# First-MoE weights: the low word's shift as a scaled copy on ScalarE, the gates' low halves subtracted on VectorE

## Chip, cores and metric

One core of one Trainium2 chip. The metric is the device time of one execution in microseconds (us), the median of several runs; lower is better. Engines are named as the profile names them: PE is the matrix engine (TensorE), DVE is VectorE, ACT is ScalarE, POOL is GpSimd, SP is SyncE, which here only issues DMAs.

## What is computed

An attention over four batches, then two mixtures of experts ("MoE") on its output. Cut to what matters:

```python
# attention: B, H, S, D = 4, 8, 576, 64; every query sees keys closer than 4, and all pooled keys (means of 4)
out = repeat(softmax(q_d @ k_d.T / 8) @ v_d, 4) + softmax(masked(q @ k.T / 8)) @ v
x = out.transpose(0, 2, 1, 3).reshape(2304, 512)
# first MoE: w1, w2, w3 are 512 x 768 (the gates), w_out is 768 x 512
h = np.maximum(np.maximum(x @ w1, x @ w2), x @ w3)
x = h @ w_out
# second MoE: w_in 512 x 2048, w_out 2048 x 512
h = np.maximum(x @ w_in, 0.0)
y = h * h @ w_out
```

The weights of both MoEs arrive as float64; q, k and v as float32.

## The kernel before

**Decoding a weight.** A float64 weight block of 128 x 512 is loaded as raw 64-bit words into a staging tile `raw` (pool `stg`, three buffers, line 93), and read as two 32-bit words, `low` and `high`. Five steps make two float32 tiles of it, `hi` (a value rounded to the matrix engine's format) and `lo` (what the rounding left):

- L98, DVE: `high` times 2^-112 and cut at a top value, which shifts the exponent to float32's.
- L103, DVE: `low` shifted right by 29, which leaves three bits of mantissa.
- L107, DVE: `high` shifted left by 3, or'ed with `low`.
- L111, DVE: the sign bit of `high` or'ed in. `low` is now the float32 weight.
- L122, ACT: `hi`, a copy of `low`; then L123, POOL: `lo`, the difference of `low` and `hi`. When `lo` is done the staging buffer is free, and SP, which waits for that at L94, issues the load of the third next weight. SP works through its loads in order, so the loads of q, k, v behind a waiting one wait too.

The first MoE has 24 such blocks: 18 of the gates (`g<f><g>`, f from 0 to 5, gate g from 0 to 2) and 6 of `w_out` (`o1<f>`). Each product with a weight is three matmuls (`mm3`, lines 128 to 130): hi times hi, hi times lo, lo times hi.

**Order.** The instructions of PE stand in the order of a plan written as tokens (`CFG`). The plan "first" runs the attention of batch 0 with all 18 gate weights decoded in between (`d1`), and puts in the first gate products as soon as a slice of x is there. "second" holds the gates and outputs of batch 0, the attention of batch 1, and the six `w_out` blocks; "mid" (twice) and "last" follow, and then the second MoE in six tiles. On DVE, ACT, POOL and SP a scheduler sets the order from its own estimates until "last"; from there on DVE's order is the written one too. Each engine works through its queue in order.

**Names in the rows.** `s`, `sd` are scores in PSUM, `sm` and `pd` the softmax of the windowed and the pooled part, `mx` and `sms` its maxima and sums, `pt` and `ptd` the transposed softmax, `o` the attention's output in PSUM, `x32` its sum with the pooled part (`up`), `xhi` and `xlo` its two halves. `g` is a gate's product in PSUM, `c` the running maximum over the gates (L380, L382), `hh` and `hl` its halves. Behind a name stand batch, head pair and part (`F` first blocks, `B` the others).

On POOL stand, beside L123: sums for pooling q, k, v (L193 to L195, L203, L204), softmax normalisation (L260, L261) and the low half of h (L388).

Of the kernel before, what the change touches and what calls it, by code (L numbers as in the profile page):

```python
# [8 lines left out]
F32 = mybir.dt.float32  # L9
F32R = mybir.dt.float32r  # L10
U32 = mybir.dt.uint32
U64 = mybir.dt.uint64
AF = mybir.ActivationFunctionType
ALU = mybir.AluOpType
# [4 lines left out]
P = 128  # L19
NEG = -1.0e9  # L20
REBIAS = 2.0**-112
F32_TOP = struct.unpack("f", struct.pack("I", (254 << 20) | 0xFFFFF))[0]

# The order of issue, as plans of tokens. Attention of a batch, per head pair p: l load q and k, m load v
# for pooling, p pool q and k, w pool v; per part F (first blocks) or B (the others): n load the windows of
# v, s scores and softmax, t transposes, v products with v. c loads the constants, d decodes a weight of the
# first MoE, e one of the second, k<kc> adds a slice of the first gate. G<half><f> and Y<half><d> are tiles
# of the gates and of y. In "second" and "mid" the attention is that of the next batch.
# "t0" counts the weights decoded at each step of the first tile of the second MoE; "qpool" gives the engine
# (v or p) that pools q and k of the first batch, "mult", "evac", "xlo" those of (later, first) batches.  # L30
CFG = {
    "qpool": "vvvp",
    "mult": "vp",
# [26 lines left out]
def local_global_attention__then__moe_kernel(  # L60
    ctx: ExitStack, tc: tile.TileContext, qT, kT, vP, cst, wg, wo1, wi2, wo2, out
):
    nc = tc.nc
    B, NP, _, S = qT.shape
# [18 lines left out]
    stg = ctx.enter_context(tc.tile_pool(name="stg", bufs=3))  # L83
# [3 lines left out]
        for b in range(B)  # L87
    ]

    def split_weights(items, late=False):  # L90
        work = []
        for src, name, *_ in items:
            raw = stg.tile([P, 512], U64, tag="raw", name=f"raw_{name}")
            nc.sync.dma_start(out=raw, in_=src)  # L94
            words = raw.bitcast(U32).rearrange("p (n two) -> p n two", two=2)
            work.append((words[:, :, 0], words[:, :, 1]))
        for low, high in work:
            nc.vector.tensor_scalar(  # L98
                out=high.bitcast(F32), in0=high.bitcast(F32), scalar1=REBIAS, scalar2=F32_TOP,
                op0=ALU.mult, op1=ALU.min,  # L100
            )
        for low, high in work:
            nc.vector.tensor_scalar(  # L103
                out=low, in0=low, scalar1=29, scalar2=None, op0=ALU.logical_shift_right
            )
        for low, high in work:
            nc.vector.scalar_tensor_tensor(  # L107
                out=low, in0=high, scalar=3, in1=low, op0=ALU.logical_shift_left, op1=ALU.bitwise_or
            )
        for low, high in work:  # L110
            nc.vector.scalar_tensor_tensor(  # L111
                out=low, in0=high, scalar=0x80000000, in1=low, op0=ALU.bitwise_and, op1=ALU.bitwise_or
            )
        parts = []
        for (src, name, pool, tag, bufs), (low, high) in zip(items, work):
            w = low.bitcast(F32)
            hi = pool.tile([P, 512], F32R, tag=tag, name=f"hi_{name}", bufs=bufs)
            lo = pool.tile([P, 512], F32R, tag=tag, name=f"lo_{name}", bufs=bufs)
            if late:
                nc.vector.tensor_copy(hi, w)  # L120
            else:
                nc.scalar.activation(out=hi, in_=w, func=AF.Copy)  # L122
            nc.gpsimd.tensor_tensor(out=lo, in0=w, in1=hi.bitcast(F32), op=ALU.subtract)  # L123
            parts.append((hi, lo))
        return parts

    def mm3(ps, whi, wlo, xhi, xlo, first, last):
        nc.tensor.matmul(ps, whi, xhi, start=first, stop=False)  # L128
        nc.tensor.matmul(ps, whi, xlo, start=False, stop=False)  # L129
        nc.tensor.matmul(ps, wlo, xhi, start=False, stop=last)  # L130
# [7 lines left out]
    at = ExitStack()  # L138
    ap = at.enter_context(tc.tile_pool(name="ap", bufs=2))
    ps_a = at.enter_context(tc.tile_pool(name="ps_a", bufs=4, space=PSUM))  # L140
    ps_m = p1.enter_context(tc.tile_pool(name="ps_m", bufs=4, space=PSUM, side="right"))

    const = ap.tile([P, NMASK * WIN + P], F32, name="const", bufs=1)
    mask = const[:, 0 : NMASK * WIN]
# [205 lines left out]
    w1_t = {}  # L350
    wo_pool = []
    w1_todo = [("g", f, g) for f in range(NF1) for g in range(NG)] + [("o", f, 0) for f in range(NF1)]

    def load_w1(n=2):
        keys = w1_todo[:n]
        del w1_todo[:n]
        items = [
            (wg[f, g], f"g{f}{g}", wpool, "w", 36) if kind == "g" else (wo1[f], f"o1{f}", wo_pool[0], "wo", 12)
            for kind, f, g in keys
        ]  # L360
        if items:
            w1_t.update(zip(keys, split_weights(items)))

    h_t = {}

    def gate_mm(b, h, f, g, ps, kc, first, last):
# [3 lines left out]
        ks = slice(kc * P, (kc + 1) * P)  # L370
        mm3(ps[:, 0:N], hi[:, ks], lo[:, ks], xhi[:, kc, :], xlo[:, kc, :], first, last)

    def gate_ps(b, h, f, g):
        return ps_m.tile([P, 512], F32, tag="m", name=f"g{b}{h}{f}{g}")

    def gate_max(b, h, f, g, ps, c):
        N = HALF[h][1] * QB
# [14 lines left out]
    def gate_unit(b, h, f):  # L392
        c = None
        for g in range(NG):
            ps = gate_ps(b, h, f, g)
            for kc in range(NP):
                gate_mm(b, h, f, g, ps, kc, kc == 0, kc == NP - 1)
            c = gate_max(b, h, f, g, ps, c)

    def y_unit(b, h, d):  # L400
        N = HALF[h][1] * QB
        ps = ps_m.tile([P, 512], F32, tag="m", name=f"yp{b}{h}{d}")
        for f in range(NF1):
            hi, lo = w1_t["o", f, 0]
            ds = slice(d * P, (d + 1) * P)
            mm3(ps[:, 0:N], hi[:, ds], lo[:, ds], h_t[b, h, f][0], h_t[b, h, f][1], f == 0, f == NF1 - 1)
        ys = tmp.tile([P, 320], F32, tag="c", name=f"ys{b}{h}{d}")[:, 0:N]
        nc.scalar.activation(out=ys, in_=ps[:, 0:N], func=AF.Copy)
        nc.scalar.dma_start(out=yscr[b][h][:, d, :], in_=ys)
# [4 lines left out]
    def act_on(b, token):  # L414
# [4 lines left out]
        elif kind == "c":  # L419
            nc.sync.dma_start(out=const, in_=cst)  # L420
        elif kind == "m":
            att_load_v(b, p)
        elif kind == "n":
            att_load_w(b, p, part)
        elif kind == "p":
            att_pool(b, p)
        elif kind == "w":
            att_pool_v(b, p)
        elif kind == "s":
            att_scores(b, p, part)  # L430
        elif kind == "t":
            att_trans(b, p, part)
        elif kind == "v":
            att_pv(b, p, part)
            vdone.add((b, p, part))
        elif kind == "d":
            load_w1(p)
        elif kind == "G":
            assert all(states[0, i].get("fdone") for i in range(NP))
            assert token[1] == "0" or len(vdone) == 2 * NP  # L440
            gate_unit(0, int(token[1]), int(token[2]))
        elif kind == "k":
            assert states[0, p]["fdone"]
            kc_done.append(p)
            for g in range(NG):
                gate_mm(0, 0, 0, g, g0[g], p, len(kc_done) == 1, len(kc_done) == NP)
                if len(kc_done) == NP:
                    c0[0] = gate_max(0, 0, 0, g, g0[g], c0[0])

    w2_t = {}  # L450
    w2_todo = [(kind, f) for f in range(NF2) for kind in ("i", "o")]

    def load_w2(n=1):
        keys = w2_todo[:n]
        at = 2 * NF2 - len(w2_todo)
        del w2_todo[:n]
        items = []
        for i, (kind, f) in enumerate(keys):
            where = (w2, "w2", 12) if at + i < 6 else (wpool, "w", 36) if at + i < 24 else (gp, "w2", 16)
            items.append(((wi2 if kind == "i" else wo2)[f], f"{kind}2{f}", *where))  # L460
        if items:
            w2_t.update(zip(keys, split_weights(items, True)))

    yt = {}
    NT2 = NT // T2
# [22 lines left out]

    with tc.manual_schedule(engines={ENG.PE}):
        g0 = [gate_ps(0, 0, 0, g) for g in range(NG)]  # L490
        c0 = [None]
        kc_done = []
# [6 lines left out]
        def run(b, plan):  # L499
            for token in plan.split():  # L500
                kind = token[0]
                if kind == "G":
                    gate_unit(b, int(token[1]), int(token[2]))
                elif kind == "Y":
                    y_unit(b, int(token[1]), int(token[2]))
                elif kind == "e":
                    load_w2()
                elif kind == "d":
                    load_w1(1)
                else:  # L510
                    act_on(b + 1, token)
# [119 lines left out]
```

## Time and profile before

| | before |
|---|---|
| median of 3 runs | 888.01 us (887.69 to 888.41) |
| span of the profiled execution | 886.9 us |
| PE busy | 834.2 us, 94% of the span |
| DVE busy | 492.7 us, 56% |
| ACT busy | 265.7 us, 30% |
| POOL busy | 238.8 us, 27% |
| chain that ended last | PE 76%, DVE 18%, issue 3%, the rest 1% or less each |

The profile is of one execution. The shares are means over stages with different limits: PE is all but full after the first sixth of the span, and DVE is full inside it. The chain is followed back from the last instruction, at each step to what released it.

### The profile page before, as it was taken

The numbers are of one execution on the slowest core, as the hardware profiler recorded it, in microseconds if no ns is written. First come the engines' busy times: TensorE is split into PE (matmuls) and PEld (weight loads), VectorE is DVE, ScalarE is ACT, GpSimd is POOL, SyncE is SP. The second block draws the span as 40 slices with busy tenths as digits, with TensorE's granted clock in tenths as the row PEclk, the third lists the DMA queues.
The fourth block names the chain that finished last, engine by engine and source line by source line (L and its number), as shares of the span: only waits on it lengthen the run. The fifth ranks groups of instructions, "written<-read, shape, count | busy, mean of one in ns | idle before, by whom it ended". The sixth has DMA issues, their size and how long they took to land.

```text
span 886.9 us, 15362 instructions
## 1 busy us (share of the span) xinstructions
PE 834.2 (94%) x6160; PEld 770.2 (87%) x6160; DVE 492.7 (56%) x944; ACT 265.7 (30%) x645; POOL 238.8 (27%) x278
## 2 busy tenths in 40 slices
PE   5558987999999999998998999999999999999998
PEld 4447986999999999998998888889989998999896
DVE  7999998633764256668679986223223223222222
ACT  3334333322343123421112434223223223223222
POOL 4877674520433005024124433001001001000000
PEclk9678999999999999999999999999999999999999
DMA  7634543320223002134235432002001001000000
GB/s 239 188 116 120 158 146 111 108 75 1 70 84 98 25 29 79 30 98 139 89 99 167 136 121 91 0 1 69 3 1 54 19 0 54 1 1 36 1 1 36
DMA packets 39831, 64.15 MB, mean 72 GB/s; under 512 B 4464, under 2 KB 23760, under 8 KB 39760
## 3 DMA queue, kind: packets, MB, share of 16 engines
q1 hardware_dynamic: 35152, 58.46, 21.2%
q10 hardware_dynamic: 4608, 4.72, 1.6%
q8 instruction: 48, 0.79, 0.4%
q14 instruction: 23, 0.19, 0.1%
HBM read 53.73 MB, written 9.44 MB: 71 GB/s over the span
## 4 chain that ended last, share of the span: by engine, by line
PE 76%; DVE 18%; issue 3%; DMA 1%; POOL 1%; ACT 1%; SPq 0%; DVEq 0%; POOLq 0%
PE po L130 7%; PE po L129 7%; PE po L128 7%; PE i L128 7%; PE i L130 7%; PE i L129 7%; PE g L128 6%; PE g L130 6%; PE g L129 6%; PE yp L128 2%; PE yp L129 2%; PE yp L130 2%; DVE raw_o L107 1%; DVE raw_g L103 1%; DVE raw_g L111 1%
## 5 line engine op out<-in xcount | busy, mean ns | idle before, releaser
L128 PE MATMUL g<-xhi,hi_g 128*128 128x256 f32 (+1 forms) x576 | 175.7, 305 | 7.8 <-DVE c L382 7.8
L129 PE MATMUL g<-xlo,hi_g 128*128 128x256 f32 (+1 forms) x576 | 172.8, 300 | 5.0 <-DVE xlo L346 5.0
L130 PE MATMUL g<-xhi,lo_g 128*128 128x256 f32 (+1 forms) x576 | 172.8, 300 | 0.0
L542 DVE TENSOR_TENSOR g<-r 128x384 f32<-128x384 f32 x80 | 45.9, 574 | 193.5 <-ACT r L540 193.5
L128 PE MATMUL i<-yh,hi_i 128*128 128x384 f32 x384 | 130.2, 339 | 0.0
L130 PE MATMUL i<-yh,lo_i 128*128 128x384 f32 x384 | 129.8, 338 | 0.0
L129 PE MATMUL i<-yl,hi_i 128*128 128x384 f32 x384 | 129.8, 338 | 0.0
L128 PEld LDWEIGHTS g<-xhi,hi_g 128*128 128x128 f32 x576 | 111.1, 193 | 10.9 <-DVE c L382 9.5
L130 PE MATMUL po<-hi_o,gl 128*128 128x512 f32 x288 | 114.6, 398 | 2.3 <-DVE gl L548 2.3
L129 PEld LDWEIGHTS g<-xlo,hi_g 128*128 128x128 f32 x576 | 111.3, 193 | 5.5 <-DVE xlo L346 5.5
L540 ACT ACTIVATE r<-i 128x384 f32<-128x384 f32 x96 | 47.1, 491 | 226.5 <-PE i L130 226.5
L128 PE MATMUL po<-hi_o,gh 128*128 128x512 f32 x288 | 114.0, 396 | 0.7 <-ACT gh L547 0.7
L129 PE MATMUL po<-lo_o,gh 128*128 128x512 f32 x288 | 114.4, 397 | 0.0
L130 PEld LDWEIGHTS g<-xhi,lo_g 128*128 128x128 f32 x576 | 110.8, 192 | 0.0
L548 DVE TENSOR_TENSOR gl<-g,gh 128x384 fp32r<-128x384 f32 x96 | 54.6, 569 | 54.1 <-ACT gh L547 53.5
L382 DVE TENSOR_TENSOR c<-g,c 128x256 f32<-128x256 f32 (+1 forms) x96 | 43.5, 453 | 65.9 <-PE g L130 64.9
L484 POOL TENSOR_TENSOR yl<-yr,yh 128x384 fp32r<-128x384 f32 x24 | 26.5, 1123 | 196.7 <-ACT yh L483 196.7
L128 PEld LDWEIGHTS i<-yh,hi_i 128*128 128x128 f32 x384 | 72.6, 189 | 4.3
L129 PEld LDWEIGHTS i<-yl,hi_i 128*128 128x128 f32 x384 | 72.6, 189 | 4.2
L130 PEld LDWEIGHTS i<-yh,lo_i 128*128 128x128 f32 x384 | 72.4, 189 | 0.0
L130 PEld LDWEIGHTS po<-hi_o,gl 128*128 128x128 f32 x288 | 54.3, 189 | 17.7 <-DVE gl L548 5.0
L547 ACT ACTIVATE gh<-g 128x384 fp32r<-128x384 f32 x96 | 50.4, 525 | 47.8 <-DVE g L542 46.2
(1055 smaller groups left out, 1410.4 us busy)
## 6 DMA issues: line engine op xcount, KB each, us to landing
raw_o<-in_wo SPq DMA_DIRECT2D x22, 512.0 KB
raw_g<-in_wg SPq DMA_DIRECT2D x18, 512.0 KB
raw_i<-in_wi SPq DMA_DIRECT2D x16, 512.0 KB
k<-in_kT SPq DMA_DIRECT2D x16, 291.0 KB
q<-in_qT SPq DMA_DIRECT2D x16, 288.0 KB
v<-in_vP SPq DMA_DIRECT2D x32, 144.0 KB
out_y<-ob SPq DMA_DIRECT2D x18, 256.0 KB
vw<-in_vP SPq DMA_DIRECT2D x16, 175.0 KB
```

The source lines that it names most:

```text
L103: nc.vector.tensor_scalar(out=low, in0=low, scalar1=29, scalar2=None, op0=ALU.logical_shift_right)
L107: nc.vector.scalar_tensor_tensor(out=low, in0=high, scalar=3, in1=low, op0=ALU.logical_shift_left, op1=ALU.bitwise_or)
L111: nc.vector.scalar_tensor_tensor(out=low, in0=high, scalar=0x80000000, in1=low, op0=ALU.bitwise_and, op1=ALU.bitwise_or)
L128: nc.tensor.matmul(ps, whi, xhi, start=first, stop=False)
L129: nc.tensor.matmul(ps, whi, xlo, start=False, stop=False)
L130: nc.tensor.matmul(ps, wlo, xhi, start=False, stop=last)
L382: nc.vector.tensor_tensor(out=c, in0=ps[:, 0:N], in1=c, op=ALU.max)
L484: nc.gpsimd.tensor_tensor(out=lo[:, kc], in0=raw[:, kc - k0], in1=hi[:, kc].bitcast(F32), op=ALU.subtract)
L540: nc.scalar.activation(out=r, in_=ps[:, 0:T2], func=AF.Relu)
L542: nc.vector.tensor_tensor(out=g, in0=r, in1=r, op=ALU.mult)
L547: nc.scalar.activation(out=ghi, in_=g, func=AF.Copy)
L548: nc.vector.tensor_tensor(out=glo, in0=g, in1=ghi.bitcast(F32), op=ALU.subtract)
```

## The change

The diff, cut to its core (comments, line moves and a helper for PSUM tiles are left out; `split_weights` becomes `split_mid` for the first MoE and `split_late` for the second):

```diff
+LOW_BITS = 0.9375 * 2.0**-29
...
-        for low, high in work:
-            nc.vector.tensor_scalar(
-                out=low, in0=low, scalar1=29, scalar2=None, op0=ALU.logical_shift_right
-            )
...
+    def low_bits(out, low):
+        nc.scalar.activation(out=out, in_=low, func=AF.Copy, scale=LOW_BITS)
...
+    def split_mid(items):
+        parts = []
+        work = [raw_words(src, name) for src, name, *_ in items]
+        for (src, name, pool, tag, bufs), (low, high) in zip(items, work):
+            rebias(high)
+            low_bits(low, low)
+            join(low, high, low)
...
+            nc.scalar.activation(out=hi, in_=w, func=AF.Copy)
+            eng = nc.gpsimd if wo_pool else nc.vector
+            eng.tensor_tensor(out=lo, in0=w, in1=hi.bitcast(F32), op=ALU.subtract)
```

For the 24 weights of the first MoE, the shift on DVE (L103) becomes a copy on ACT with a scale and integers at both ends (L104 of the new kernel): the scale brings the 32-bit word to 0 to 7.5. It reads only the raw word, so it need not wait for L98; the join behind it (L107) waits for ACT. `wo_pool` is empty through the plan "first", so the 18 gate subtractions go to DVE (L126), and the 6 of `w_out` stay on POOL. The 32 weights of the second MoE are decoded as before.

PE's order is the same. The scheduler's order on the others changes up to about 145 us of the old trace, and is the same from there on. The old line L122 is L124 now, L123 is L126, L111 is L110; attention lines are 22 higher, gate lines 25.

DVE, first three gate weights. Before:

```order
L111 SCALAR_TENSOR_TENSOR raw_g00_154<-raw_g00_154 128x512
L98 TENSOR_SCALAR raw_g02_193<-raw_g02_193 128x512
L103 TENSOR_SCALAR raw_g02_193<-raw_g02_193 128x512
L256 TENSOR_REDUCE sms02F_252<-sm02F_234 128x4
L107 SCALAR_TENSOR_TENSOR raw_g01_175<-raw_g01_175 128x512
L258 RECIPROCAL sms01F_221<-sms01F_221 128x6
L107 SCALAR_TENSOR_TENSOR raw_g02_193<-raw_g02_193 128x512
L338 TENSOR_TENSOR x3200F_332<-o00F_315,up00_328 128x256
L257 TENSOR_SCALAR sms02F_252<-sms02F_252 128x6
L111 SCALAR_TENSOR_TENSOR raw_g01_175<-raw_g01_175 128x512
```

and after:

```order
L110 SCALAR_TENSOR_TENSOR raw_g01_175<-raw_g01_175 128x512
L107 SCALAR_TENSOR_TENSOR raw_g02_193<-raw_g02_193 128x512
L279 TENSOR_SCALAR sms02F_252<-sms02F_252 128x6
L126 TENSOR_TENSOR lo_g00_161<-raw_g00_154,hi_g00_160 128x512
L360 TENSOR_TENSOR x3200F_332<-o00F_315,up00_328 128x256
L110 SCALAR_TENSOR_TENSOR raw_g02_193<-raw_g02_193 128x512
L280 RECIPROCAL sms02F_252<-sms02F_252 128x6
L126 TENSOR_TENSOR lo_g01_182<-raw_g01_175,hi_g01_181 128x512
L258 SCALAR_TENSOR_TENSOR sm03F_336<-s03F_338,const_92 128x280
L266 TENSOR_REDUCE mx03F_353<-sd03F_347 128x2
L368 TENSOR_TENSOR xlo00_331<-x3200F_332,xhi00_330 128x256
L126 TENSOR_TENSOR lo_g02_200<-raw_g02_193,hi_g02_199 128x512
```

The shifts have gone, and each weight's subtraction stands among the attention's steps, before the slice `xlo00` that PE waits for.

ACT, between the transposes of head pairs 1 and 2. Before:

```order
L268 ACTIVATE ptd01F_383<-td01F_390 72x512
L247 ACTIVATE pd03F_337,sms03F_354<-sd03F_347,mx03F_353 128x144 x2
L255 ACTIVATE sm03F_336<-sm03F_336 128x280
L122 ACTIVATE hi_g10_289<-raw_g10_283 128x512
L247 ACTIVATE pd00B_402,sms00B_418<-s00B_403,mx00B_417 128x144
```

and after:

```order
L290 ACTIVATE ptd01F_383<-td01F_390 72x512
L104 ACTIVATE raw_g10_283<-raw_g10_283 128x512
L269 ACTIVATE pd03F_337,sms03F_354<-sd03F_347,mx03F_353 128x144 x2
L104 ACTIVATE raw_g11_305<-raw_g11_305 128x512
L277 ACTIVATE sm03F_336<-sm03F_336 128x280
L104 ACTIVATE raw_g12_367<-raw_g12_367 128x512
L124 ACTIVATE hi_g10_289<-raw_g10_283 128x512
L350 ACTIVATE up01_465<-o01F_452 128x96
L290 ACTIVATE pt02F_485<-t02F0_487 70x512
L269 ACTIVATE pd00B_402,sms00B_418<-s00B_403,mx00B_417 128x144
```

Three scaled copies now stand ahead of the exponential `pd00B`, each of which needs its raw load to have landed.

DVE, weights g40 to g42, after (before, L123 on POOL stood where L126 stands, and freed the staging buffer):

```order
L98 TENSOR_SCALAR raw_g40_620<-raw_g40_620 128x512
L407 TENSOR_TENSOR c002_897<-g0022_913,c002_897 128x256
L107 SCALAR_TENSOR_TENSOR raw_g40_620<-raw_g40_620 128x512
L98 TENSOR_SCALAR raw_g41_687<-raw_g41_687 128x512
L126 TENSOR_TENSOR lo_g32_615<-raw_g32_608,hi_g32_614 128x512
L360 TENSOR_TENSOR x3201B_947<-o01B_931,up01_465 128x320
L110 SCALAR_TENSOR_TENSOR raw_g40_620<-raw_g40_620 128x512
L107 SCALAR_TENSOR_TENSOR raw_g41_687<-raw_g41_687 128x512
L368 TENSOR_TENSOR xlo01_864<-x3201B_947,xhi01_863 128x320
L110 SCALAR_TENSOR_TENSOR raw_g41_687<-raw_g41_687 128x512
L126 TENSOR_TENSOR lo_g40_627<-raw_g40_620,hi_g40_626 128x512
L98 TENSOR_SCALAR raw_g42_697<-raw_g42_697 128x512
```

Weight g42 is loaded into the buffer that `lo_g32` frees seven rows before DVE wants it.

## Rows read from the trace of the kernel before

**Rows 1.** Stretches: length, busy PE, PEld, DVE, ACT, POOL; PEclk, DMA share, GB/s.

```profile
14.50:64.30 49.80, 28.80 (x284) 22.59 (x283) 49.77 (x82) 17.75 (x49) 41.44 (x48) 0.73 0.50 153
64.30:95.90 31.60, 27.05 (x293) 25.10 (x295) 31.50 (x54) 13.35 (x37) 22.29 (x22) 0.84 0.48 146
95.90:147.00 51.10, 42.95 (x369) 40.09 (x365) 49.83 (x95) 17.30 (x44) 34.02 (x33) 1.00 0.42 135
147.00:390.00 243.00, 242.65 (x2552) 233.06 (x2553) 128.91 (x324) 78.56 (x235) 64.01 (x108) 0.99 0.20 61
390.00:887.00 497.00, 486.00 (x2598) 443.87 (x2596) 224.50 (x375) 135.94 (x277) 72.34 (x56) 0.99 0.17 53
```

**Rows 2.** Waits of PE, 0 to 200 us: us in total, times, longest.

```profile
PE g L129 <- DVE xlo L346: 5.0, 2, 2.9
...
PE s01B L221 <- ACT pd00B L247: 4.4, 1, 4.4
PE g L128 <- DVE c L382: 4.2, 3, 1.7
PE t10B L284 <- DVE x3210F L338: 3.9, 1, 3.9
PE t03B L284 <- ACT pt02B L268: 3.1, 1, 3.1
```

**Rows 3.** Groups of DVE, 14.5 to 147 us: busy us, mean ns | idle before.

```profile
L107 DVE SCALAR_TENSOR_TENSOR raw_g<-raw_g 128x512 uint32<-128x512 uint32 x18 | 15.8, 878 | 0.0
L103 DVE TENSOR_SCALAR raw_g<-raw_g 128x512 uint32<-128x512 uint32 x18 | 14.1, 784 | 0.0
...
L103 DVE TENSOR_SCALAR raw_o<-raw_o 128x512 uint32<-128x512 uint32 x6 | 4.6, 766 | 0.0
```

**Rows 4.** Single lines' rows: duration ns min/median/max, first and last start us.

```profile
L103 DVE TENSOR_SCALAR raw_g<-raw_g x18: 412/548/1932, 16.0 to 104.2; 128x512 uint32<-128x512 uint32 x18
L107 DVE SCALAR_TENSOR_TENSOR raw_g<-raw_g x18: 673/862/1674, 17.7 to 107.0; 128x512 uint32<-128x512 uint32 x18
L122 ACT ACTIVATE hi_g<-raw_g x18: 661/678/696, 20.3 to 112.8; 128x512 fp32r<-128x512 f32 x18
```

**Rows 5.** Group of POOL, 14.5 to 147 us.

```profile
L123 POOL TENSOR_TENSOR lo_g<-raw_g,hi_g 128x512 fp32r<-128x512 f32 x18 | 26.4, 1466 | 15.8 <-ACT hi_g L122 15.8
```

**Rows 6.** DVE in order of time: start us, us, instruction [idle before <-releaser].

```profile
23.38 2.35 DVE L257 TENSOR_SCALAR sms02F<-sms02F 128x6 f32<-128x6 f32 x1
...
108.90 0.16 DVE L257 TENSOR_SCALAR sms11F<-sms11F 128x6 f32<-128x6 f32 x1
109.51 0.78 DVE L98 TENSOR_SCALAR raw_o<-raw_o 128x512 f32<-128x512 f32 x1 [0.46 <-POOL qd L195]
...
113.64 1.73 DVE L107 SCALAR_TENSOR_TENSOR raw_o<-raw_o 128x512 uint32<-128x512 uint32 x1
```

**Rows 7.** POOL in order of time, the first and last gate subtraction.

```profile
23.81 1.28 POOL L123 TENSOR_TENSOR lo_g<-raw_g,hi_g 128x512 fp32r<-128x512 f32 x1
...
113.51 1.30 POOL L123 TENSOR_TENSOR lo_g<-raw_g,hi_g 128x512 fp32r<-128x512 f32 x1 [1.34 <-ACT hi_g L122]
```

**Rows 8.** Waits of SP, 0 to 150 us: us in total, times, longest.

```profile
SPq L94 <- POOL lo_g L123: 43.4, 17, 5.6
```

**Rows 9.** SP in order of time: a load of a staging buffer.

```profile
105.80 0.33 SPq L94 DMA_DIRECT2D raw_o<-in_wo  x1
```

**Rows 10.** PE, DVE and ACT in order of time, around 80 us.

```profile
77.41 0.80 PE L309 MATMUL o01B<-pt01B,vw 70*64 70x64 f32 x20
...
80.84 0.41 DVE L382 TENSOR_TENSOR c<-g,c 128x256 f32<-128x256 f32 x1
...
81.29 0.42 ACT L386 ACTIVATE hh<-c 128x256 fp32r<-128x256 f32 x1 [2.73 <-DVE c L382]
...
81.70 0.74 ACT L268 ACTIVATE pt02B<-t02B 70x512 f32<-70x512 f32 x2
...
82.43 1.04 PE L284 MATMUL t03B<-const,sm03B 128*70 128x128 f32 x4 [3.11 <-ACT pt02B L268]
```

More of the change, by code (lines that the diff above doesn't have):

```diff
@@ L88, in local_global_attention__then__moe_kernel, with raw_words @@
     ]
[L90 to L96, printed above, removed]
-        for low, high in work:
-            nc.vector.tensor_scalar(
-                out=high.bitcast(F32), in0=high.bitcast(F32), scalar1=REBIAS, scalar2=F32_TOP,
-                op0=ALU.mult, op1=ALU.min,
-            )
-        for low, high in work:
+    def raw_words(src, name):
+        raw = stg.tile([P, 512], U64, tag="raw", name=f"raw_{name}")
+        nc.sync.dma_start(out=raw, in_=src)
+        words = raw.bitcast(U32).rearrange("p (n two) -> p n two", two=2)
+        return words[:, :, 0], words[:, :, 1]
@@ new lines, in rebias, with join @@
+    def rebias(high):
+        nc.vector.tensor_scalar(
+            out=high.bitcast(F32), in0=high.bitcast(F32), scalar1=REBIAS, scalar2=F32_TOP,
+            op0=ALU.mult, op1=ALU.min,
+        )
+    def low_bits(out, low):
+        nc.scalar.activation(out=out, in_=low, func=AF.Copy, scale=LOW_BITS)
+    def join(out, high, bits):
+        nc.vector.scalar_tensor_tensor(
+            out=out, in0=high, scalar=3, in1=bits, op0=ALU.logical_shift_left, op1=ALU.bitwise_or
+        )
+        nc.vector.scalar_tensor_tensor(
+            out=out, in0=high, scalar=0x80000000, in1=out, op0=ALU.bitwise_and, op1=ALU.bitwise_or
+        )
@@ new lines, in split_mid @@
+    def split_mid(items):
[5 more added lines that the diff above has]
+            join(low, high, low)
+            hi = pool.tile([P, 512], F32R, tag=tag, name=f"hi_{name}", bufs=bufs)
+            lo = pool.tile([P, 512], F32R, tag=tag, name=f"lo_{name}", bufs=bufs)
+            w = low.bitcast(F32)
+            nc.scalar.activation(out=hi, in_=w, func=AF.Copy)
+            eng = nc.gpsimd if wo_pool else nc.vector
+            eng.tensor_tensor(out=lo, in0=w, in1=hi.bitcast(F32), op=ALU.subtract)
+            parts.append((hi, lo))
+        return parts
@@ L103, in split_weights, with split_late @@
+    def split_late(items):
+        parts = []
+        work = [raw_words(src, name) for src, name, *_ in items]
+        for low, high in work:
+            rebias(high)
             nc.vector.tensor_scalar(
@@ L105, in split_weights @@
             )
[L106 to L114, printed above, removed]
+            join(low, high, low)
         for (src, name, pool, tag, bufs), (low, high) in zip(items, work):
@@ L118, in split_weights @@
             lo = pool.tile([P, 512], F32R, tag=tag, name=f"lo_{name}", bufs=bufs)
[L119 to L122, printed above, removed]
+            nc.vector.tensor_copy(hi, w)
             nc.gpsimd.tensor_tensor(out=lo, in0=w, in1=hi.bitcast(F32), op=ALU.subtract)
@@ L361, in load_w1 @@
         if items:
-            w1_t.update(zip(keys, split_weights(items)))
+            w1_t.update(zip(keys, split_mid(items)))
     h_t = {}
@@ L371, in gate_mm, with mm_ps @@
         mm3(ps[:, 0:N], hi[:, ks], lo[:, ks], xhi[:, kc, :], xlo[:, kc, :], first, last)
+    def mm_ps(name):
+        return ps_m.tile([P, 512], F32, tag="m", name=name)
     def gate_ps(b, h, f, g):
-        return ps_m.tile([P, 512], F32, tag="m", name=f"g{b}{h}{f}{g}")
+        return mm_ps(f"g{b}{h}{f}{g}")
     def gate_max(b, h, f, g, ps, c):
@@ L401, in y_unit @@
         N = HALF[h][1] * QB
-        ps = ps_m.tile([P, 512], F32, tag="m", name=f"yp{b}{h}{d}")
+        ps = mm_ps(f"yp{b}{h}{d}")
         for f in range(NF1):
@@ L461, in load_w2 @@
         if items:
-            w2_t.update(zip(keys, split_weights(items, True)))
+            w2_t.update(zip(keys, split_late(items)))
     yt = {}
```

## Prediction, written before the changed kernel ran

> **What bounds the kernel now.** I read the stretches of the span first, since the shares of the whole mix stages. From 147 us on PE is full: 242.65 of 243.00 us until 390, and 486.00 of 497.00 us after that [rows 1]. Before that it isn't: from 14.5 to 147 us it idles 49.80 - 28.80 = 21.0 us, then 31.60 - 27.05 = 4.6 us, then 51.10 - 42.95 = 8.2 us, 33.7 us together, and in the same three stretches DVE is busy 49.77 of 49.80, 31.50 of 31.60 and 49.83 of 51.10 us [rows 1]. I call them stretches A, B and C. DVE is the bound there. The waits of PE say the same: those on `xlo`, `c` and `x3210F` end with a DVE instruction, and those that end with ACT (`pd00B`, `pt02B`) have DVE results behind them [rows 2]. What leaves DVE's queue before 147 us can bring PE's full part forward by as much, up to PE's idle time in each stretch, and nothing in the later part has to change for that.
>
> The second thing to see is why DVE is so slow there. A `tensor_scalar` over 128x6 values takes 0.16 us at 108.90 and 2.35 us at 23.38 [rows 6]. The long one begins during POOL's work and runs while POOL's first gate subtraction, 23.81 to 25.09, does [rows 7]. So it is with the last: the DVE row at 113.64 takes 1.73 us, where the shortest of its kind takes 0.673 [rows 4, 6], and POOL's subtraction lies at 113.51 to 114.81 [rows 7]. I took each DVE row's time beyond the shortest of its form, and how much of that lies under a POOL row. Over 227 DVE rows from 14.5 to 147 us the excess is 47.2 us. Each of the 18 gate subtractions lies under the excess of exactly one DVE row, 18.5 us in all: 8.9 in A (8 of them), 6.6 in B (6) and 3.0 in C (4); rows 6 and 7 show the first and the last pair.
>
> **The change part by part.**
>
> *Shifts leave DVE.* 24 of them. In the stretch they take 14.1 + 4.6 = 18.7 us [rows 3], but their shortest is 0.412 us [rows 4], and what is above that is POOL's doing and will hit another DVE row if only the shift goes. So I count 24 x 0.415 = 10.0 us off.
>
> *18 subtractions come to DVE.* The old trace has none of this size there. The nearest row is L107: as many elements, two SBUF inputs, 0.673 us at the shortest and 0.878 us as a mean with its stalls [rows 3, 4]. I take 0.68, as the stalls are counted by POOL's rows: 18 x 0.68 = 12.2 us on; the upper end is 18 x 0.878 = 15.8.
>
> The Trainium skill's page "VectorE: DVE Perf Modes" (The perf-mode tier table) speaks against the change at this point: an operation with one source may run at twice the rate in float32, one with two tensors may not, so a cheap instruction is swapped for a dear one. The rows agree, 0.412 against 0.673 us; by that rule alone DVE would get 12.2 - 10.0 = 2.2 us more work.
>
> *18 subtractions leave POOL.* They take 26.4 of POOL's 41.44 + 22.29 + 34.02 = 97.8 us in the three stretches, 27% [rows 1, 5]. If all POOL work were alike, DVE would be rid of 27% of 47.2 us, 12.7 us; by the pairs it is rid of 18.5. I take 18.5, since none of the 18 ran without holding DVE up. Relief of zero is excluded only if the remaining POOL rows don't stall DVE more than now; that is a rival below.
>
> *By stretch.* A: 8 x (0.68 - 0.415) - 8.9 = -6.8. B: seven weights, 7 x 0.265 - 6.6 = -4.7. C: nine shifts and three subtractions, -3.7 + 2.0 - 3.0 = -4.7. Sum -16.2 us on DVE. PE can take up 21.0, 4.6 and 8.2. B just about fits: 3.1 us of its idle time is `t03B` [rows 2], which waits for `pt02B` on ACT, which stands behind `hh` (81.29), which waits for `c` on DVE (80.84) [rows 10]. The products that `c` reads are done by 77.41, when PE goes on to `o01B`, and PE has work until 82.43 - 3.11 = 79.32 [rows 10]. The chain of 0.41 + 0.42 + 0.74 us fits into that, so this wait can go. Lost to the bound in B: 0.2.
>
> *Scaled copies on ACT.* 24 x 0.678 us = 16.3 us, by the row of `hi`, which has the same shape [rows 4]. ACT is busy 17.75 + 13.35 + 17.30 = 48.4 us of 132.5 [rows 1]; with these, 64.7 of about 117, 55%. The cover is ACT's own idle time, and the copy needs no DVE result, so it can run while DVE does L98 or earlier work. Without cover DVE stands before L107 for the copy's 0.678 less L98's 0.415, 0.26 us a weight, 6.3 us in all. In the old trace the raw words had landed before DVE came for them (no idle time before L103, and 0.46 us once before L98 [rows 3, 6]), so I take 1 us of 0 to 6.3. Queued behind L107 is all of DVE's attention work, and PE waits for that.
>
> *The staging buffer is freed by DVE.* SP issues the next load when `lo` is done; that wait stays, on DVE where it was POOL [rows 8]. A load issued at 105.80 was used at 109.51 [rows 6, 9], so it takes at most 3.7 us. In the new order the rows between `lo_g32` and the L98 of g42, which uses its buffer, are four of L107's size, 4 x 0.68 = 2.7 us, and two shorter ones, so 3 to 4 us, and four neighbours stand as close. Each may wait 0 to 1 us: 0 to 5, and I take 2. Loads of q, k and v queue behind these on SP as before.
>
> *POOL's other work* comes earlier, since its queue is shorter by 26.4 us. No price: it is off the path once DVE's inputs are there.
>
> **Sum.** -16.2 + 0.2 + 1 + 2 = -13.0 us. The profiled execution has 886.9 us from first to last instruction, and the median is 888.0, so 1.1 us lie outside or between runs. 886.9 - 13.0 + 1.1 = **875.0 us**.
>
> **The rivals.**
>
> *New waits eat most of it.* Both waits at their upper ends, 6.3 + 5 = 11.3 us in the place of 3: -16.2 + 0.2 + 11.3 = -4.7, **883.3**. For: stretch B is tight on DVE and on the loads. Against: three staging buffers, and ACT idle two thirds of the time.
>
> *The stalls move instead of going.* POOL's remaining 97.8 - 26.4 = 71.4 us get denser against a shorter DVE stretch, and the new DVE rows have two SBUF inputs and can be held up themselves. At half the relief, 9.2 us: 2.2 - 9.2 + 3 = -4.0, **884**; with none, 893. Against: without the shifts there are fewer such rows on DVE than before (24 out, 18 in).
> The Trainium skill's page "SBUF — State Buffer" (Who interferes with whom) is behind this rival: a DVE instruction with two SBUF inputs and a GpSimd instruction that reads SBUF exclude each other, and whoever issues first keeps the pair to its end. Rows 6 and 7 agree with the exclusion; by the rule the 18 new rows stall and are stalled as L107 is.
>
> *Slower: ACT's queue is held by a copy that waits for its load.* In the new order three scaled copies stand ahead of `pd00B`, on which PE's `s01B` waits 4.4 us already [rows 2]. ACT works in order, so a late load stops the exponentials and transposes behind the copy, and DVE and PE after them. It decides from 16.2 / 18 = 0.9 us for each gate weight; at 1.2 us it is 21.6 - 16.2 = +5.4, **893.4**. Against: loads had landed ahead of use in the old trace, and copies of the next weight stand one or two weights ahead.
>
> *More comes back.* No new waits, and a busier PE keeps its clock: the granted clock is 0.73 in A and 0.84 in B, and 1.00 in C [rows 1]. 0.84 is 32% of B at 1.2 GHz; at 2.4 GHz the work in that part, 0.32 x 27.05 = 8.7 us, would take half, 4.3 less. -16.2 - 4.3 = -20.5, **867.5**.
>
> **How the numbers follow.** Forecast 875.0, 870 to 881 on its own, 0.55. New waits 0.15, stalls move 0.12, more comes back 0.12, slower 0.06. The range from 867 to 884.5 leaves out the slower rival and the worse ends of two others, some 0.17. A measurement of this kernel tells 0.2%, 1.8 us, from no change. Faster by more: 0.55 + 0.12, and 0.13 and 0.08 of the two rivals near 884, 0.88; within it 0.05; slower 0.07.
>
> **What would show it.** Right: PE's full part begins near 134 us where it began at 147; the DVE rows from 14.5 us on with fewer long ones, L107 with a mean near 0.78 us; the subtraction at 0.68 us at its shortest; DVE still at 95% or more until then. Wrong: idle time of DVE before L107 that ends with ACT, or before L98 that ends with a load (new waits); the excess over the shortest rows still near 47 us (stalls move); ACT idle before the scaled copies, ended by a load (slower). The stretch after it should have its old length; if it hasn't, the reasoning that only the start matters is wrong.

## Result, and the profile after

The changed kernel takes 876.69 us, median of 4 runs (876.09 to 878.28), beside 888.21 us (887.69 to 889.09) for the kernel before on the same chip: ratio 0.9869, 95% interval [0.9852, 0.9886], 11.5 us less. The forecast was 875.0, within 867 to 884.5. The profiled execution has a span of 876.4 us, 10.5 less than the 886.9 before; the spans of the four runs are 874.2 to 876.4, so it is the longest of them.

The same five stretches, after (length, busy PE, PEld, DVE, ACT, POOL; PEclk, DMA share, GB/s):

```profile
14.50:64.30 49.80, 33.49 (x318) 27.28 (x319) 49.61 (x98) 26.09 (x66) 30.60 (x39) 0.97 0.52 156
64.30:95.90 31.60, 27.96 (x325) 26.12 (x323) 28.32 (x56) 16.96 (x43) 12.21 (x16) 0.84 0.53 164
95.90:147.00 51.10, 47.99 (x417) 45.81 (x414) 44.91 (x93) 22.29 (x56) 33.16 (x37) 0.97 0.43 130
147.00:390.00 243.00, 241.93 (x2523) 232.77 (x2521) 132.26 (x318) 77.19 (x228) 66.53 (x105) 1.00 0.21 65
390.00:887.00 497.00, 475.02 (x2517) 432.64 (x2515) 213.79 (x359) 132.74 (x270) 66.19 (x51) 0.99 0.15 49
```

Against [rows 1], PE is busy for 4.7, 0.9 and 5.0 us more in A, B and C, POOL for 10.8, 10.1 and 0.9 us less, ACT for 16.9 us more in all. The long stretch from 147 to 390 us is as full as it was. The whole gain lies ahead of it, and it can be read at one DVE row: `x3210F`, the last result of DVE that holds PE up in the old trace (`t10B`, 3.9 us [rows 2]), began at 146.43 us and now begins at 135.40:

```profile
135.40 0.42 DVE L360 TENSOR_TENSOR x3210F<-o10F,up 128x256 f32<-128x256 f32 x1 [0.75 <-ACT up L350]
```

That is 11.0 us earlier. From its end to the end of the span it was 740.0 us and is 740.6.

The groups of DVE from 14.5 to 138 us (busy us, mean ns | idle before, and what ended it), for [rows 3]:

```profile
L126 DVE TENSOR_TENSOR lo_g<-raw_g,hi_g 128x512 fp32r<-128x512 f32 x18 | 14.9, 830 | 0.8 <-ACT hi_g L124 0.8
...
L107 DVE SCALAR_TENSOR_TENSOR raw_g<-raw_g 128x512 uint32<-128x512 uint32 x18 | 14.1, 781 | 0.0
L98 DVE TENSOR_SCALAR raw_g<-raw_g 128x512 f32<-128x512 f32 x18 | 11.2, 622 | 0.2 <-DMA raw_g<-in_wg 0.2
```

and single lines (min/median/max ns, first and last start), for [rows 4]:

```profile
L126 DVE TENSOR_TENSOR lo_g<-raw_g,hi_g x18: 649/682/2135, 23.7 to 102.8; 128x512 fp32r<-128x512 f32 x18
L104 ACT ACTIVATE raw_g<-raw_g x18: 667/680/731, 14.4 to 93.5; 128x512 uint32<-128x512 uint32 x18
L107 DVE SCALAR_TENSOR_TENSOR raw_g<-raw_g x18: 677/685/1219, 16.1 to 96.5; 128x512 uint32<-128x512 uint32 x18
```

L107 is the same instruction on the same data as before. Its mean fell from 878 to 781 ns and its longest row from 1674 to 1219, with the shortest unchanged (673 and 677): it is held up less.

**An account of DVE.** For each kernel I split the time from DVE's first row that starts at 14.0 us or later to the end of `x3210F` in three: *idle* (gaps between rows), *excess* (each row's time beyond the shortest of its line and form in that trace, summed) and *work* (the rest). All numbers but the last column are from the one profiled execution; "rest" is from there to the end of the span, "ratio" is to the kernel before by the timed runs.

| kernel | work | excess | idle | end of `x3210F` | rest | ratio |
|---|---|---|---|---|---|---|
| before | 83.8 | 47.6 | 1.4 | 146.9 | 740.0 | 1 |
| changed | 85.1 | 29.6 | 6.5 | 135.8 | 740.6 | 0.9869 |
| shift moved only | 76.6 | 43.7 | 7.3 | 141.7 | 738.8 | 0.9907 |
| subtractions moved only | 93.6 | 27.7 | 9.1 | 144.4 | 740.6 | 0.9949 |
| all 24 subtractions on DVE | 88.6 | 27.0 | 4.2 | 133.8 | 740.1 | 0.9814 |
| + 18 POOL rows | 87.6 | 36.2 | 4.1 | 141.9 | 737.8 | 0.9904 |
| + 36 POOL rows | 86.8 | 39.3 | 5.7 | 145.8 | 739.5 | 0.9974 |
| + 18 ACT rows | 85.2 | 30.7 | 5.8 | 135.7 | 737.7 | 0.9853 |
| + softmax products on DVE | 88.1 | 29.2 | 7.2 | 138.5 | 739.4 | 0.9901 |
| all of it on DVE | 93.4 | 20.3 | 10.2 | 138.0 | 740.6 | 0.9896 |

For the change: work +1.3, excess -18.0, idle +5.1, together -11.6 (the first row counted began 0.5 us later, so the end came 11.0 earlier). Counted from the first L98 row in both kernels instead, it is work +2.0, excess -17.6, idle +5.1.

### The profile page after: what moved, and what is told of

It reads as the page before. It is cut to its first block, busy times and chain, and to the rows that moved or that the text cites. A ratio compares the mean times of both kernels' runs of the same rounds, so it can differ in the third digit from the quotient of the medians.

```text
span 876.4 us, 15330 instructions
## 1 busy us (share of the span) xinstructions
PE 833.2 (95%) x6160; PEld 770.2 (88%) x6160; DVE 477.7 (55%) x938; ACT 278.6 (32%) x669; POOL 214.0 (24%) x260
## 4 chain that ended last, share of the span: by engine, by line
PE 83%; DVE 10%; DMA 3%; issue 1%; ACT 1%; POOL 0%; SPq 0%; DVEq 0%; ACTq 0%; POOLq 0%
PE g L149 8%; PE g L150 8%; PE g L151 7%; PE po L151 7%; PE po L150 7%; PE po L149 7%; PE i L149 7%; PE i L151 7%; PE i L150 7%; PE yp L149 3%; PE yp L151 3%; PE yp L150 3%; DMA q<-in_qT 1%; DMA raw_g<-in_wg 1%; DVE lo_g L126 1%
## 5 line engine op out<-in xcount | busy, mean ns | idle before, releaser
L407 DVE TENSOR_TENSOR c<-g,c 128x256 f32<-128x256 f32 (+1 forms) x96 | 43.6, 455 | 69.2 <-PE g L151 67.4
```

Of the source, the lines that this page charges most:

```text
L407: nc.vector.tensor_tensor(out=c, in0=ps[:, 0:N], in1=c, op=ALU.max)
```

## Experiments

My theory is the prediction's: DVE bounds the start, the gain is POOL's subtractions no longer holding DVE's rows up, and the added ACT work is covered. The rivals are that the halves don't work as priced, that POOL's rows were not the cause, that ACT is not covered, or that another engine has become the bound.

No edit changes one thing alone, since the scheduler then sets new orders on DVE, ACT and POOL: about 185 of the changed kernel's first 241 DVE rows keep their order among each other in the kernel with 18 POOL rows more, 193 in the one with 18 ACT rows more, and 97 to 129 in those with one half of the change or with the softmax products moved.

**Each half alone.** First the shift moved to ACT, the subtractions left on POOL:

```diff
-            eng = nc.gpsimd if wo_pool else nc.vector
+            eng = nc.gpsimd
```

> The changed kernel with the 18 gate subtractions back on POOL, so the shift on ScalarE alone. Theory (the gain is POOL's 18 subtractions no longer stalling DVE, and the shifts' undisturbed 0.415 us each): DVE loses 10.0 us of work before 147 us and keeps the stalls of 18.5 us, new waits 1 to 3 us; 888.2 - 10 + 2 = about 880, 878 to 883. Rival (the shifts were the whole of it, 18.7 us with their stalls): 870 to 873.

Measured: 881.62 us (880.4 to 882.25), ratio 0.9907 [0.9893, 0.9922]. Then the subtractions moved to DVE, the shift left there:

```diff
-        nc.scalar.activation(out=out, in_=low, func=AF.Copy, scale=LOW_BITS)
+        nc.vector.tensor_scalar(
+            out=out, in0=low, scalar1=29, scalar2=None, op0=ALU.logical_shift_right
+        )
```

> The changed kernel with the shift back on DVE, so the gates' subtractions on DVE alone. Theory: +12.2 us of subtractions, -18.5 us of stalls, waits 1 to 3: 888.2 - 6.3 + 2 = about 884, 881 to 887; DVE's time over its shortest rows before the full part of PE falls from 47 us to about 29. Rival (stalls move to other POOL rows): the excess stays above 40 us and the time is 890 or more.

Measured: 884.74 us (884.5 to 886.71), ratio 0.9949 [0.9934, 0.9964]. Both halves gain, as 0.93% + 0.51% = 1.44% beside 1.31% [1.14, 1.48] for both, so by the times they add within the measurement. In the profiled executions `x3210F` comes 5.2 and 2.5 us earlier, 7.7 together beside 11.0 for both (the profiled run of the second is the longest of its four by 2.0 us), so how exactly they add stays open. The account says what each is worth on the kernel before: the shift's move takes 7.2 us of work and 3.9 of excess off DVE and adds 5.9 of idle time, the subtractions' move takes 19.9 us of excess off at the price of 9.8 us of work and 7.7 of idle time. With the shift already moved, the subtractions' move takes only 14.1 us of excess off, for 8.5 of work. The second half alone lets DVE idle 9.1 us, and here its waits show on what (DVE, us in total, times, longest):

```profile
DVE raw_o L98 <- DMA raw_o<-in_wo: 3.6, 3, 1.7
DVE raw_g L98 <- DMA raw_g<-in_wg: 2.8, 3, 1.6
```

This is the landing of the raw words that the prediction priced at 0 to 5 us. In the changed kernel it is 0.2 us on DVE for the gates (the row of L98 above), and ACT, which now reads the raw word too, waits for the loads (lines that end ACT's idle time before L104, us and times, in the changed kernel):

```profile
  DMA raw_g<-in_wg: 14.6, 10
  DMA raw_o<-in_wo: 5.7, 5
```

So the two halves carry different terms, and together they lack a wait that the second brings alone. That ACT takes this wait over is my reading; the last kernel below has ACT's copies and DVE waiting for loads as well.

**The last six subtractions to DVE as well.**

```diff
-            eng = nc.gpsimd if wo_pool else nc.vector
+            eng = nc.vector
```

> The changed kernel with the six subtractions of w_out on DVE as well. Theory: 6 x 0.68 = 4.1 us more on DVE, 4.6 us of stalls under POOL's six rows gone: 876.7 -0.5, 874 to 879. Rival (DVE is no longer the bound there, PE is): no change within 0.2%, and DVE idle. Rival (stalls move): 879 to 882.

Measured: 873.67 us (872.11 to 875.68), ratio 0.9814 [0.9795, 0.9833]. A little more than expected (874 to 879), and the fastest kernel of this study: 16.0 us under the kernel before. Its work is 3.5 us above the changed kernel's, excess and idle are 2.6 and 2.3 us below. The gain here is as much in DVE's waits as in the stalls.

**More work on POOL.** If POOL's rows are the cause, rows that do nothing else should bring the loss back. For each gate weight, one or two subtractions whose result nobody reads:

```diff
+            if not wo_pool:
+                N = HALF[1][1] * QB
+                junk = hp.tile([P, N], F32R, tag="hl15", name=f"junk_{name}")
+                nc.gpsimd.tensor_tensor(
+                    out=junk, in0=hi[:, 0:N].bitcast(F32), in1=hi[:, 0:N].bitcast(F32), op=ALU.subtract
+                )
```

> The changed kernel with 18 added POOL subtractions of 128x320, one per gate weight, that read hi alone and write a tile nobody reads: POOL's load back, DVE's work as changed. Theory (every such POOL row holds DVE up by about 0.7 to 1.0 us): 876.7 + 12 to 18 = 887 to 894. Rival (the stalls are not of POOL's work): 876.7 +- 2.

Measured: 881.24 us (880.51 to 881.71), ratio 0.9904 [0.9889, 0.9919], about 3 to 4.5 us over the changed kernel. I had expected 12 to 18 us, so the size was a miss. The account shows which part holds: excess +6.6, and `x3210F` 6.1 us later. The rows took 17.8 us of POOL, with 0.71 us at the shortest where a gate's subtraction of 128x512 took 1.28 [rows 7], so they were worth 0.37 us of DVE's excess for each us of POOL, and the old ones 14.1 to 19.9 us for 26.4, 0.53 to 0.75. And 2.8 us were given back behind `x3210F` (last section). The same with two of them:

> The changed kernel, with two subtractions of 128x320 on POOL for each of the 18 gate weights, where the run before had one; nobody reads their result. With one, 17.8 us of POOL work brought 6.4 us more excess of the DVE rows over their shortest, and the start of the program became 6.1 us longer. Theory (POOL's rows hold DVE's rows up in proportion to POOL's time): excess 11 to 14 us above the changed kernel's 29.8, start 11 to 14 us longer, whole time some 9 to 14 us above it, ratio to the kernel before 0.997 to 1.003. Rival (the first run's loss came from POOL's own queue, as its softmax products come later): a longer wait of PE for POOL's products, and DVE's excess hardly above the 36 us of the run with one.

Measured: 886.85 us (885.77 to 888.92, 10 runs), ratio 0.9974 [0.9964, 0.9984]. The time is as expected, the start is 10.0 us longer and the excess 9.7 us larger, both a bit less than the 11 to 14 expected. The excess isn't proportional to POOL's time: the first 18 rows brought 6.6 us, the second 18 3.1. The rival's sign is there too, but small: PE waits 5.7 us for POOL's product `sm03F`, as it does with 18 rows, where it waits 4.0 in the changed kernel. Unread POOL work, 35.4 us where the change had taken 26.4 off, thus brings back most of what the change gained. That the new order alone did it is unlikely: the ACT rows below reorder the queues about as much, and `x3210F` moved by 0.1 us. A row of DVE and the three POOL rows that it lies under, from the kernel with 18 rows:

```profile
59.59 2.13 DVE L110 SCALAR_TENSOR_TENSOR raw_g<-raw_g 128x512 uint32<-128x512 uint32 x1
```
```profile
59.34 0.77 POOL L288 TENSOR_TENSOR sm01B<-sm01B,sms01B 128x350 f32<-128x350 f32 x1
60.06 0.43 POOL L289 TENSOR_TENSOR pd01B<-pd01B,sms01B 128x144 f32<-128x144 f32 x1
60.45 0.72 POOL L130 TENSOR_TENSOR junk_g<-hi_g 128x320 fp32r<-128x320 f32 x1
```

POOL is done at 61.17, and 0.55 us later so is DVE's row, which takes 0.67 us at the shortest. That POOL pays too is seen in the same kernel, where DVE has seven short rows one after the other from 37.66 to 40.63:

```profile
38.01 2.35 POOL L130 TENSOR_TENSOR junk_g<-hi_g 128x320 fp32r<-128x320 f32 x1
```

With 36 rows POOL's own rows are 35.4 - 36 x 0.712 = 9.8 us longer than at their shortest. In the first case POOL was at work when DVE's row began, in the second DVE was when POOL's began, and the one at work went on with its next rows. Why these rows cost DVE less for each us than the old subtractions did isn't settled.

**More work on ACT.**

```diff
+            if not wo_pool:
+                N = HALF[1][1] * QB
+                junk = hp.tile([P, N], F32R, tag="hl15", name=f"junk_{name}")
+                nc.scalar.activation(out=junk, in_=hi[:, 0:N].bitcast(F32), func=AF.Copy)
```

> The changed kernel, with one more ACT copy of 128x320 for each of the 18 gate weights, behind the copy that makes the high half; its result is read by nobody. It asks whether ACT's idle time really covers the 24 scaled copies. ACT is busy 26.09 + 16.96 + 22.29 = 65.3 us of the 132.5 in the three stretches of the changed kernel; 18 x about 0.45 us add some 8. Theory (ACT has cover, the copies cost nothing there): at most 2 us over the changed kernel, ratio to the kernel before 0.987 to 0.990. Rival (ACT's order is a bound already, and what the change gains is lessened by its copies): 6 us or more over it, ratio 0.994 or more.

Measured: 875.8 us (875.22 to 875.87), ratio 0.9853 [0.9837, 0.987]. 8.4 us more of ACT cost nothing: `x3210F` ends at 135.7 where it was 135.8. So ACT's busy time doesn't bound the start, and that rival falls; what a copy costs that waits for its load, with others behind it, this run doesn't test. It also tells of the clock in A: its row shows 0.63 there, where the changed kernel has 0.97,

```profile
14.50:64.30 49.80, 31.76 (x302) 25.40 (x303) 49.22 (x96) 28.79 (x73) 28.50 (x39) 0.63 0.52 154
```

and the start is as long.

**POOL's softmax products.** After the change, PE has a wait that it hadn't (waits of PE, 0 to 200 us: in total, times, longest):

```profile
PE t03F L306 <- POOL sm03F L282: 4.0, 1, 4.0
PE t03B L306 <- ACT pt02B L290: 3.6, 1, 3.6
```

A wait of this kind was there before, and [rows 2], which begin with the second longest, leave it out; it is 1.3 us now:

```profile
PE t01F L284 <- POOL sm01F L260: 5.1, 1, 5.1
```

Without the subtractions POOL's order has pooling sums ahead of that product. The edit moves the eight products to DVE, by the table "mult" of the plan:

```diff
-    "mult": "vp",
+    "mult": "vv",
```

> The changed kernel with the eight softmax products that POOL still made (batch 0's and others of 128x280 and 128x350) on DVE. In the changed kernel PE has a new wait of 4.0 us for the last of POOL's first four products, which stood behind pooling sums there. By that wait alone: 4 us less in stretch A, and another 1.3 us at the wait before it. Against it, DVE gets 4 to 8 rows of 0.44 to 0.55 us, 2 to 4 us, and POOL's rows of the same work no longer hold DVE's up (3.1 us of excess lie under them now). Theory (DVE is still the bound of the start, whoever PE is seen to wait for): -3 to +1 us against the changed kernel, ratio 0.983 to 0.988. Rival (POOL's queue has become the bound of stretch A): -4 us or better, ratio 0.982 or less.

Measured: 880.06 us (878.27 to 882.02), ratio 0.9901 [0.9883, 0.9919], about 3 us over the changed kernel, outside the theory's upper end (+1 us) and far from the rival's. The waits that it was to remove got longer:

```profile
PE t03F L306 <- DVE sm03F L282: 7.6, 1, 7.6
PE t01F L306 <- DVE sm01F L282: 4.9, 1, 4.9
```

DVE in order of time shows why. One row stands in front, and takes 4.45 us where its form takes 0.41; then five more stand ahead of the product:

```profile
39.52 4.45 DVE L368 TENSOR_TENSOR xlo<-x3201F,xhi 128x256 fp32r<-128x256 f32 x1
...
46.16 0.44 DVE L282 TENSOR_TENSOR sm03F<-sm03F,sms03F 128x280 f32<-128x280 f32 x1
```

Under the long row POOL runs without a gap, eight rows of pooling and softmax from 38.91 to 43.68; the first and the last:

```profile
38.91 1.17 POOL L225 TENSOR_TENSOR v<-v 72x256 f32<-72x256 f32 x1
...
43.13 0.55 POOL L217 TENSOR_TENSOR kd<-kd,k 128x144 f32<-128x144 f32 x1
```

POOL's rival as the bound of A falls, and so does the hope that less POOL work is always less stall: the order on POOL counts too.

**Both moves together.** All 24 subtractions and the eight products on DVE.

> Both moves on top of the change: all 24 subtractions of the first stage's weights and the eight softmax products on DVE. The 24 subtractions alone gave a ratio of 0.981, about 4.5 us less than the changed kernel. If the two add, with -1 us for the products: 0.980, about 871 to 874 us. If POOL's queue was the bound: 0.977 or less. If DVE is now so full that each further row costs its time: 0.983 to 0.986.

Measured: 879.75 us (878.2 to 880.88), ratio 0.9896 [0.9881, 0.9911], 6 to 7 us slower than with the subtractions alone, and slower than any of the three values I had given. The excess falls to 20.3 us, the lowest of all, but work rises to 93.4 and idle to 10.2, of which 5.4 us are L98 waiting for its load. Excess alone isn't the goal; the sum of the three is.

## Why the prediction was right, step by step

**DVE as the bound of the start: right.** In the ten kernels the end of `x3210F` moves by 13.1 us, and what follows stays at 737.7 to 740.6 us. In B it was right of the kernel before only: the changed kernel's DVE is busy 28.32 of 31.60 us there, not the 95% I named as a sign.

**Shifts off, 10.0 us, and subtractions on, 12.2 us: right as a difference, each too large.** Shortest durations of 0.649 us (L126) beside 0.68 are close. But rows of DVE overlap their neighbours by some 0.1 us, so that the 24 shifts filled 8.0 us of the queue and the 18 subtractions fill 10.3: +2.3 where I had +2.2. In the table work rose 1.3, as some attention rows counted before run ahead of 14.0 us after; from the first L98 row on it rose 2.0.

**Relief of 18.5 us: right for the change as a whole, and partly by luck.** Excess fell by 18.0 in the changed kernel. But the subtractions' move took off 19.9 on the kernel before and 14.1 with the shift already moved, the second nearer the proportional estimate of 12.7. The pairs weren't as clean as I had them either: three of the 18 subtractions lie under the excess of two rows, and the one at 102.99 us meets just 0.15 us of excess; with the larger row of each the sum is still 18.7. The rival that the stalls move instead falls with this: L107's mean of 0.78 us was the sign named.

**Join waits 1 us, landing 2 us: the sum too small, and in other places.** There is no idle time before L107 (2.5 us with the shift alone) and 1.1 us before L98. DVE idles 5.1 us more all the same. It waits (10 to 150 us, some of it behind `x3210F`; in total, times, longest):

```profile
DVE c L407 <- PE g L151: 2.4, 5, 0.8
DVE xlo L368 <- ACT xhi L366: 1.2, 2, 0.9
...
DVE raw_i L98 <- DMA raw_i<-in_wi: 0.9, 1, 0.9
```

Relieved of stalls DVE comes to wait for PE and ACT, which the sum had as nothing. With 5.1 in the place of 3, -13.0 becomes -10.9, and `x3210F` came 11.0 earlier: this is the term that was mis-sized. The other terms were off by less than 1 us each, in both directions.

**"This wait can go" (`t03B` in B): wrong.** It is 3.6 us where it was 3.1 [rows 2]. The products for `c` do come in time, by 71.8 us, but neither DVE nor ACT then goes on as the sum had it. On DVE `c` stands behind three held rows, 3.7 us from the first's start to its own, where their shortest are 0.48, 0.68 and 0.41:

```profile
70.98 2.07 DVE L368 TENSOR_TENSOR xlo<-x3200B,xhi 128x320 fp32r<-128x320 f32 x1
72.97 1.26 DVE L110 SCALAR_TENSOR_TENSOR raw_g<-raw_g 128x512 uint32<-128x512 uint32 x1
74.15 0.65 DVE L98 TENSOR_SCALAR raw_g<-raw_g 128x512 f32<-128x512 f32 x1
74.71 0.41 DVE L407 TENSOR_TENSOR c<-g,c 128x256 f32<-128x256 f32 x1
```

Then on ACT, in order of time:

```profile
75.64 0.68 ACT L104 ACTIVATE raw_g<-raw_g 128x512 uint32<-128x512 uint32 x1 [0.59 <-DMA raw_g<-in_wg]
76.22 0.40 ACT L411 ACTIVATE hh<-c 128x256 fp32r<-128x256 f32 x1
76.53 0.74 ACT L290 ACTIVATE pt02B<-t02B 70x512 f32<-70x512 f32 x2
```

A scaled copy waits 0.59 us for its load and runs 0.68, and `hh` and `pt02B` stand behind it. Of PE's 3.64 us, from 73.61 on, 1.5 pass until `c` is done, 1.1 more until `hh` starts, and 1.0 in `hh` and `pt02B`. The copy's part is the mechanism of my slower rival, and it shows at a second place, the one that this rival named: PE's `s01B` waits 3.0 us for `pt02F`, whose input was there by 32.7 us, and which stood behind a copy that waited 2.14 us for its load:

```profile
34.58 0.67 ACT L104 ACTIVATE raw_g<-raw_g 128x512 uint32<-128x512 uint32 x1 [2.14 <-DMA raw_g<-in_wg]
...
35.83 0.60 ACT L290 ACTIVATE pt02F<-t02F 70x512 f32<-70x512 f32 x1
```

DVE didn't wait for ACT or PE anywhere in A, so there this cost PE, not the bound. Over the start ACT waited 20.3 us for such loads, the longest 2.9. I had named such waits as the sign of a slower kernel; they came, and the kernel is faster, so the sign was a poor one. Measured at PE, the gain was 5.7 us behind A's last slice (`o00B` at 65.55 where it was 71.27), 5.8 after B (`s10B` at 95.04, was 100.84), 6.3 at `t10B`, and 11.9 when its long wait was gone (`s12B` at 139.17, was 151.09). DVE's gain in B reached PE only in C.

**Clock: no gain from it, as forecast, but a loss in B that I hadn't looked for.** A's granted clock went from 0.73 to 0.97, and the run with more ACT work, with 0.63 and the same start, shows that nothing hung on it there. B's stayed at 0.84. In both kernels PE works at the lower of its levels (1.2 and 2.4 GHz) behind its wait for `t03B`, and that wait stayed: the granted clock is 0.50 from 82 to 86 us before, and now

```profile
78.00:82.00 4.00, 4.00 (x40) 3.46 (x39) 4.00 (x7) 2.37 (x7) 1.51 (x2) 0.50 0.53 166
82.00:86.00 4.00, 4.00 (x20) 4.00 (x20) 2.46 (x5) 1.95 (x6) 0.00 (x0) 0.50 0.74 196
```

These 8 us are worth up to 4 us of PE's work at the higher level. Right behind, at 86.0 and 87.6 us, DVE waits 0.7 and 0.8 us for gate products of PE. So some of the idle time of DVE may be PE's clock, and not only DVE's lead; no run here tells how much.

**Later stretch unchanged: right to 0.6 us** in the profiled executions, the 0.6 partly by luck, since it differs by up to 2.9 us among the ten. The change's 11.0 us became 10.5 in the span and 11.5 in the medians.

## What to carry to other kernels

Where VectorE bounds a stretch and GpSimd works beside it, compare each VectorE row with the shortest of its form, and look at which GpSimd row lies under the difference: here moving 18 GpSimd rows onto the busier engine cost it 8.5 to 9.8 us of work and took 14 to 20 us of stalls off it. Judge a move by work, stalls and idle time together, since the kernel with the fewest stalls was 6 to 7 us slower than the best. Before a step that waits for a load goes to an engine with spare time, look at what stands behind it in that engine's queue: here ACT could take 16 us of copies and 20 us of waiting, and PE waited for what stood behind a copy at two places.

## What the runs showed of the hardware

**One held row can outlast a whole series of GpSimd rows.** I had paired one subtraction with one VectorE row. With the shift moved alone, a row over 128x6 values takes 4.55 us:

```profile
22.63 4.55 DVE L279 TENSOR_SCALAR sms02F<-sms02F 128x6 f32<-128x6 f32 x1
```
```profile
22.11 1.31 POOL L226 TENSOR_TENSOR vd<-v 72x128 f32<-72x128 f32 x2
23.39 0.65 POOL L282 TENSOR_TENSOR sm01F<-sm01F,sms01F 128x280 f32<-128x280 f32 x1
24.00 0.66 POOL L283 TENSOR_TENSOR pd01F<-pd01F,sms01F 128x288 f32<-128x288 f32 x1
24.62 2.53 POOL L126 TENSOR_TENSOR lo_g<-raw_g,hi_g 128x512 fp32r<-128x512 f32 x2
```

It ends with the last of them, at 27.2. Between these rows of POOL, DVE's did not get in.

**Not every VectorE row is held.** From 14.5 to 140 us in the changed kernel, 75 rows that reduce or have a source in PSUM (L258, L266, L273, L278, L360, L407) have 0.8 us of excess together, though half of their time lies under a row of POOL (17.1 of 33.5 us); the other 156 rows have 29.0. The Trainium skill's page "SBUF — State Buffer" (Who interferes with whom) says that reductions, and rows with at most one SBUF input outside the two-port modes, don't contend with GpSimd; this case's rows agree.

**The clock dips later in the span, in places that differ.** In the second MoE's first tiles PE has short waits, and after some the granted clock is low for a few us. Two windows of the changed kernel, then three of the one with 18 POOL rows more:

```profile
396.00:400.00 4.00, 2.46 (x9) 2.46 (x10) 3.35 (x8) 0.42 (x1) 1.29 (x1) 0.59 0.57 151
400.00:404.00 4.00, 4.00 (x19) 4.00 (x18) 3.29 (x8) 0.91 (x2) 1.31 (x1) 0.56 0.29 111
```
```profile
400.00:404.00 4.00, 1.34 (x10) 1.08 (x9) 3.79 (x6) 0.00 (x0) 1.72 (x2) 1.00 0.76 228
472.00:476.00 4.00, 3.46 (x10) 2.41 (x9) 3.96 (x5) 1.06 (x3) 2.69 (x2) 0.68 0.33 100
476.00:480.00 4.00, 4.00 (x20) 3.68 (x20) 3.90 (x7) 0.84 (x2) 1.79 (x2) 0.90 0.51 173
```

With levels of 1.2 and 2.4 GHz, 0.59 and 0.56 are 3.3 and 3.5 us at the lower one, worth up to 3.4 us of work. In the other kernel the wait is as long (2.7 us from 400 to 404; 2.8 us from 392 to 400 in the changed kernel), and no dip follows there, but one of 3.4 us near 475 us does. So dips explain up to 1.7 of the 2.8 us by which that kernel's rest is shorter, and PE idles 1.3 us less in it. The kernel with more ACT work has no dip at all behind `x3210F`, and with 737.7 us the shortest rest. This is why differences of under 3 us between two profiled executions aren't read here without the start's account. What decides whether a dip follows stays open.
